# A gated dynamic convolution with a two-product layer behind it: the order of the first block's work, a load from another queue, and a third slot filled by copies

## The chip, the cores and the metric

The kernel runs on one core of a Trainium2 chip. The metric is the device time of one execution in microseconds; lower is better. Engines are named TensorE (PE, with its weight loads as PEld), VectorE (DVE), ScalarE (ACT), GpSimd (POOL) and SyncE (SP), which issues most DMAs.

## The reference, cut to what matters

```python
# x (4, 4096, 192), weight_gen (4, 4096, 8, 7): a causal convolution of 7 taps, its weights by token and head
w = exp(weight_gen - max(weight_gen, axis=-1))
w = w / (sum(w, axis=-1) + 1e-09)
x_pad = concatenate([zeros((B, 6, D)), x], axis=1)
out[b, s, h, g] = sum_k w[b, s, h, k] * x_pad[b, s + k, h, g]
# on the 16384 tokens
h = out.reshape(16384, 192) @ w_in            # w_in (192, 2048)
g = where(h >= 1, h, where(h <= -1, 0, (h + 1) ** 2 / 4))
result = g @ w_out                            # w_out (2048, 192)
```

The two weight matrices come as 64-bit floats; the kernel decodes them on the chip.

## The kernel before, in words

**Tiling.** The 16384 tokens are cut into 32 blocks of 512. A block's convolution works on a tile of 128 partitions by 4 tokens (L179, L189), so a product of one tap is an operation on 128x768. The result is turned so that the 192 channels lie on partitions, 64 to a row half: three slots c = 0, 1, 2 of 64 channels, each held twice, once in the lower and once in the upper 64 partitions, so that a pair of matmuls can work on both row halves at once. For blocks 0 and 1 slot c holds channels c*64 to c*64+127 of a row that is lengthened by its first 64 channels, and `gemm1_pair` (L378) takes the weights of slot (c + h) % 3 for row half h.

**Precision.** Every operand is split into a high and a low part (`hc`, `hl` for the activations, `whi`, `wlo` and both halves of `wo` for the weights): ScalarE copies the high part (L258, L352), VectorE or GpSimd subtracts the low part (L259, L356). The first product is 18 matmuls for a pair of 128-column slices (three slots, three passes, two row halves), the second 32 for each half.

**Order.** The whole program is under a manual schedule: each engine and each queue works in the order in which the code issues. A pair w (two slices of the 2048 hidden columns) goes through `gemm1_pair`, ScalarE's `relu` and `square` (L389, L392), VectorE's minimum and maximum `act_g` (L397), the split `split_g` (L403, L404) and, two pairs later, `gemm2_part` (L432) in two parts. A block has 8 pairs.

**The prologue** (L532 to L575). SyncE issues the loads of the softmax weights for groups 0 (block 0) and 1 (blocks 1 and 2) and the load of x for block 0 (L126, and L129 for the first two partitions, whose first rows are the zero padding that GpSimd clears at L119). `softmax` (L149 to L155) is seven operations; those of groups 0 and 1 are interleaved, with group 1's subtraction and last multiplication on GpSimd. `marks` collects instructions on which others are made to wait: the first load of the weight matrices (chunk 0 of 8, L308 and L314) waits for group 0's addition of 1e-9. `drive` (L208) keeps TensorE at work with 13 matmuls that nobody reads. `conv_summed` makes block 0's convolution as five tiles (`piece`): taps 0 and 4, 5, 6 alone, taps 1 to 3 summed on VectorE in PSUM. VectorE reads the softmax weights from a copy in PSUM (`near`, made by ScalarE, L224), GpSimd from SBUF. `again` (L169) copies a piece's first 64 channels behind its end. TensorE then turns and sums the pieces (`turn_sum`, L267): 5 pieces, 3 slots and 4 turns each, 60 in all. `split_x` makes the high and low parts of the three slots, and the first weight chunk is decoded by `cast_act`, `cast_dve`, `merge`, `high` and `low` (L327, L331, L340, L352, L356).

**After it.** `first_pairs` and `early_pair` decode one chunk for each pair while block 0 is computed; block 1's convolution runs on GpSimd in between (`wave`), each operation held until a chunk's decoding has been issued. At the last pair of block 0 (w = 7) block 1's result is turned: slots 0 and 1 before the second product's part 0, and in `edge_pair`, between the parts, slot 2. From block 2 on the turning goes over VectorE's transposition (L284) and DRAM. Block 2's convolution stands on GpSimd's queue from pair 6 on (two operations), its transposition on VectorE's at pair 11, ahead of that pair's `act_g`.

## Time and profile before

| | |
|---|---|
| median of 3 runs | 1161.32 us (1160.6 to 1161.62) |
| span of the profiled execution, first to last instruction | 1158.6 us |
| the median less this span, what lies around it | 2.7 us |
| TensorE busy | 1145.0 us, 12885 matmuls |
| VectorE, ScalarE, GpSimd busy | 834.1, 964.7, 792.5 us |
| TensorE busy from 10 to 20, 20 to 30, 50 to 60 us | 8.67, 7.01, 8.95 of 10 us |

The profiled execution is known by its span alone; its own time is put at the span and the 2.7 us around it. Busy times are of single engines that work beside each other. The span of the profile begins with the first instruction, and all places in time below are microseconds from there.

### The profile page before, as it was taken

The numbers are of one execution on the slowest core, as the hardware profiler recorded it, in microseconds if no ns is written. First come the engines' busy times: TensorE is split into PE (matmuls) and PEld (weight loads), VectorE is DVE, ScalarE is ACT, GpSimd is POOL, SyncE is SP. The second block draws the span as 40 slices with busy tenths as digits, with TensorE's granted clock in tenths as the row PEclk, the third lists the DMA queues.
The fourth block names the chain that finished last, engine by engine and source line by source line (L and its number), as shares of the span: only waits on it lengthen the run. The fifth ranks groups of instructions, "written<-read, shape, count | busy, mean of one in ns | idle before, by whom it ended". The sixth has DMA issues, their size and how long they took to land.

```text
span 1158.6 us, 32197 instructions
## 1 busy us (share of the span) xinstructions
PE 1145.0 (99%) x12885; PEld 1038.1 (90%) x12885; DVE 834.1 (72%) x1271; ACT 964.7 (83%) x1745; POOL 792.5 (68%) x511
## 2 busy tenths in 40 slices
PE   7999999999999999999999999999999999999998
PEld 5799999999999999999999999999999999999997
DVE  8887767677676776767777676776767767677664
ACT  6878888888888888888888888888888888888886
POOL 4788976667857678486686866678576785866310
PEclk9999999999999999999999999999999999999999
DMA  9422222212222212222121222222222122221100
GB/s 229 112 82 79 77 84 90 89 64 73 75 77 90 84 61 82 71 87 90 56 89 59 85 89 90 64 73 74 76 90 95 51 85 70 80 90 57 47 24 15
DMA packets 84052, 91.43 MB, mean 79 GB/s; under 512 B 5056, under 2 KB 75712, under 8 KB 83904
## 3 DMA queue, kind: packets, MB, share of 16 engines
q1 hardware_dynamic: 83904, 89.39, 24.0%
q8 instruction: 101, 1.65, 0.6%
q14 instruction: 47, 0.39, 0.1%
HBM read 64.99 MB, written 24.38 MB: 77 GB/s over the span
## 4 chain that ended last, share of the span: by engine, by line
PE 95%; ACT 2%; DMA 2%; DVE 1%; issue 0%; POOL 0%; DVEq 0%; POOLq 0%; ACTq 0%; SPq 0%
PE o L432 48%; PE psh L378 45%; DMA r<-in_moe_w_in_dram 1%; PE psx L267 1%; DMA r<-in_moe_w_out_dram 1%; PE psx L208 0%; ACT u L392 0%; DVE psh L397 0%; ACT u L389 0%; ACT gh L403 0%; DVE psw L340 0%; DVE gl L404 0%; POOL piece L189 0%; POOL acc L189 0%; ACT hc L258 0%
## 5 line engine op out<-in xcount | busy, mean ns | idle before, releaser
L432 PE MATMUL o<-wo,gh 64*128 64x384 f32 x4096 | 612.2, 355 | 1.5 <-SPq L441 1.4
L397 DVE SCALAR_TENSOR_TENSOR psh<-u,psh 128x512 f32<-128x512 f32 x512 | 354.7, 696 | 299.6 <-ACT u L392 299.4
L432 PE MATMUL o<-wo,gl 64*128 64x192 f32 x4096 | 542.7, 251 | 0.0
L432 PEld LDWEIGHTS o<-wo,gh 64*128 64x128 f32 x4096 | 421.1, 184 | 13.1 <-SPq L441 2.3
L432 PEld LDWEIGHTS o<-wo,gl 64*128 64x128 f32 x4096 | 421.3, 187 | 9.0
L389 ACT ACTIVATE u<-psh 128x512 f32<-128x512 f32 x512 | 301.5, 589 | 93.2 <-PE psh L378 91.2
L404 DVE TENSOR_TENSOR gl<-psh,gh 128x512 fp32r<-128x512 f32 x512 | 345.7, 686 | 15.3 <-ACT gh L403 1.1
L403 ACT ACTIVATE gh<-psh 128x512 fp32r<-128x512 f32 x512 | 299.2, 592 | 65.5 <-DVE psh L397 65.5
L378 PE MATMUL psh<-hc,whi 64*128 64x512 f32 x1536 | 349.8, 404 | 3.7 <-DVE wlo L356 1.9
L189 POOL TENSOR_TENSOR acc<-acc,pr 128x768 f32<-128x768 f32 x185 | 343.8, 1858 | 5.7 <-DVE head L331 2.0
L378 PE MATMUL psh<-hl,whi 64*128 64x512 f32 x1536 | 337.7, 391 | 0.0
L378 PE MATMUL psh<-hc,wlo 64*128 64x512 f32 x1536 | 337.3, 390 | 0.0
L392 ACT ACTIVATE u<-u 128x512 f32<-128x512 f32 x512 | 323.7, 632 | 16.0
L179 POOL TENSOR_TENSOR pr<-x,w 128x768 f32<-128x768 f32 x186 | 286.8, 1549 | 7.1 <-DVE psw L340 7.1
L259 POOL TENSOR_TENSOR hl<-XT,hc 128x512 fp32r<-128x512 f32 x90 | 115.4, 1297 | 221.2 <-ACT hc L258 221.2
L378 PEld LDWEIGHTS psh<-hl,whi 64*128 64x128 f32 x1536 | 173.6, 185 | 34.7 <-DVE hl L259 0.3
L378 PEld LDWEIGHTS psh<-hc,whi 64*128 64x128 f32 x1536 | 173.0, 185 | 29.4 <-DVE wlo L356 4.3
L378 PEld LDWEIGHTS psh<-hc,wlo 64*128 64x128 f32 x1536 | 174.1, 187 | 21.4
L179 POOL TENSOR_TENSOR acc<-x,w 128x768 f32<-128x768 f32 x31 | 47.9, 1547 | 72.5 <-DVE w L155 70.6
L258 ACT ACTIVATE hc<-XT 128x512 fp32r<-128x512 f32 x90 | 55.5, 618 | 0.0
L284 DVE STREAM_TRANSPOSE T<-acc 128x768 f32<-128x768 f32 x30 | 50.9, 1698 | 0.3 <-POOL acc L189 0.3
L457 DVE SCALAR_TENSOR_TENSOR osb<-o,osb 128x384 f32<-128x384 f32 x64 | 32.7, 556 | 2.7 <-ACT osb L456 2.7
(44 smaller groups left out, 188.8 us busy)
## 6 DMA issues: line engine op xcount, KB each, us to landing
x<-in_x_dram SPq DMA_DIRECT2D x28, 960.0 KB
XT<-D SPq DMA_DIRECT2D x180, 128.0 KB
out_dram<-osb SPq DMA_DIRECT2D x31, 384.0 KB
D<-T SPq DMA_DIRECT2D x30, 384.0 KB
x<-in_x_dram SPq DMA_DIRECT2D x4, 945.0 KB
w<-in_weight_gen_dram SPq DMA_DIRECT2D x15, 224.0 KB
r<-in_moe_w_in_dram SPq DMA_DIRECT2D x16, 192.0 KB
r<-in_moe_w_out_dram SPq DMA_DIRECT2D x8, 384.0 KB
```

Of the source, the lines that this page charges most:

```text
L179: held(eng.tensor_tensor(out=t, in0=xtile[:, k:k + n, :].rearrange("p j (h g) -> p j h g", h=H), in1=wt[:, gi, :, :, k:k + 1].to_broadcast ...
L189: held(eng.tensor_tensor(out=o, in0=s, in1=t, op=ALU.add))
L258: ops.append(lambda c=c: nc.scalar.activation(out=hc[:, c], in_=src[c], func=AF.Copy))
L259: ops.append(lambda c=c: lows.append(engines[c].tensor_tensor(out=hl[:, c], in0=src[c], in1=hc[:, c].bitcast(F32), op=ALU.subtract)))
L284: lambda: nc.vector.transpose(out=T.rearrange("p b c j -> p b j c"), in_=acc.rearrange("p j (r b) -> p b j r", b=R)),
L378: nc.tensor.matmul(out=pair[h][:, 0:N], lhsT=l[rows, f // 2, (c + h) % NC if b < 2 else c], rhs=r[rows, c], start=(s == 0), stop=(s == len ...
L389: nc.scalar.activation(out=u_t[i], in_=h_t[i][:, 0:N], func=AF.Relu, scale=0.5 * UNIT, bias=0.5)
L392: nc.scalar.activation(out=u_t[i], in_=u_t[i], func=AF.Square, scale=UNIT ** -0.5)
L397: nc.vector.scalar_tensor_tensor(out=pv, in0=uv, scalar=1.0 / UNIT, in1=pv, op0=ALU.min, op1=ALU.max)
L403: nc.scalar.activation(out=gh[:, 0:N], in_=gv, func=AF.Copy)
L404: nc.vector.tensor_tensor(out=gl[:, 0:N], in0=gv, in1=gh[:, 0:N].bitcast(F32), op=ALU.subtract)
L432: mm = nc.tensor.matmul(out=o_t[b][turn][:, k, 0:cols], lhsT=g_t[i][l][rows, t * P:(t + 1) * P], rhs=wo[rows, f].rearrange("p s d -> p (s ...
```

## The change

The prologue is put in another order and some of its steps are replaced.

- Block 0's x is cleared and loaded ahead of everything else; its large load is issued from ScalarE's queue, its two edge loads from SyncE's, and only then group 0's softmax weights. Group 1's weights are loaded behind the first chunk of the weight matrices, which now waits for group 0's subtraction.
- Group 0's softmax runs alone; its last multiplication writes `near` in PSUM, and ScalarE copies from there to SBUF for GpSimd. Group 1's softmax comes in between and behind the decoding of chunk 0 and the split of block 0.
- Block 0's convolution makes six pieces: taps 0 and 1 and the sum of 2 and 3 on VectorE, taps 4, 5, 6 on GpSimd. Each is turned for slots 0 and 1 alone, 8 turns, 48 in all. The drive has 9 matmuls.
- Slot 2 (channels 128 to 191, and 0 to 63) is filled by half-partition copies: the high part by ScalarE from the turned slots, the low part by GpSimd from the low parts of slots 0 and 1. Block 1's slot 2 is made in the same way in `edge_pair`.
- The second half of chunk 0's cast goes from VectorE to ScalarE.

```diff
@@ -118,12 +118,12 @@
         if halo(b):
             nc.gpsimd.memset(x_t[b][0:halo(b), 0:HALO, :], 0.0)
 
-    def load_x(b, edge=nc.sync):
+    def load_x(b, main=nc.sync, edge=nc.sync):
         t0, t, p0 = b * N, x_t[b], halo(b)
         src = bass.AP(
             tensor=xr.tensor, offset=xr[t0 + p0 * n - HALO:t0 + p0 * n - HALO + 1, :].offset,
             ap=[[n * D, P - p0], [1, (n + HALO) * D]])
-        nc.sync.dma_start(out=t[p0:P].rearrange("p j d -> p (j d)"), in_=src)
+        main.dma_start(out=t[p0:P].rearrange("p j d -> p (j d)"), in_=src)
         for p in range(p0):
             z = HALO - p * n
             edge.dma_start(out=t[p:p + 1, z:HALO + n, :], in_=xr[t0:t0 + (p + 1) * n, :])
@@ -137,7 +137,7 @@
             in_=wr[t0:t0 + nb * N, :].rearrange("(b p j) e -> p b (j e)", p=P, j=n))
         w_t[g] = t
 
-    def softmax(g, less=nc.vector, times=nc.vector):
+    def softmax(g, less=nc.vector, times=nc.vector, into=None):
         t = w_t[g]
         q = len(groups[g]) * n * H
         tv = t.rearrange("p b j h k -> p (b j h) k")[:, 0:q]
@@ -145,6 +145,7 @@
         s = sp.tile([P, 2 * n * H, 2], F32, tag="s", name="s")
         mv, sv = m[:, 0:q], s[:, 0:q, 0]
         mx, sx = (v.unsqueeze(2).to_broadcast([P, q, K]) for v in (mv, sv))
+        final = tv if into is None else into
         return [
             lambda: nc.vector.tensor_reduce(out=mv, in_=tv, axis=AX.X, op=ALU.max),
             lambda: less.tensor_tensor(out=tv, in0=tv, in1=mx, op=ALU.subtract),
@@ -152,7 +153,7 @@
             lambda: nc.vector.tensor_reduce(out=sv, in_=tv, axis=AX.X, op=ALU.add),
             lambda: nc.vector.tensor_scalar(out=sv, in0=sv, scalar1=1e-9, scalar2=None, op0=ALU.add),
             lambda: nc.vector.reciprocal(out=sv, in_=sv),
-            lambda: times.tensor_tensor(out=tv, in0=tv, in1=sx, op=ALU.mult),
+            lambda: times.tensor_tensor(out=final, in0=tv, in1=sx, op=ALU.mult),
         ]
 
     acc_t = {}
@@ -160,13 +161,10 @@
     SYNC = mybir.DependencyInfo(mybir.DependencyClass.Sync, mybir.DependencyReason.DATA)
 
     def whole():
-        return op.tile([P, n, D + Q], F32, tag="piece", name="piece", bufs=5)
+        return op.tile([P, n, D], F32, tag="piece", name="piece", bufs=6)
 
     def by_head(t):
-        return t[:, :, 0:D].rearrange("p j (h g) -> p j h g", h=H)
-
-    def again(t):
-        nc.scalar.activation(out=t[:, :, D:D + Q], in_=t[:, :, 0:Q], func=AF.Copy)
+        return t.rearrange("p j (h g) -> p j h g", h=H)
 
     def conv(b, eng, gate=None, into=None):
         g, gi = group_of[b]
@@ -213,38 +211,36 @@
                 before = None
 
 
-    def conv_summed(b):
+    near = ps_o.tile([P, 2, 512], F32, tag="o1", name="near")
+
+    def conv_pieces(b):
 
         g, gi = group_of[b]
-        wt, xtile = w_t[g], x_t.pop(b)
-        near = ps_o.tile([P, 2, 512], F32, tag="o1", name="near")
+        far, xtile = w_t[g][:, gi], x_t.pop(b)
         wn = near[:, 0, 0:n * E].rearrange("p (j h k) -> p j h k", j=n, h=H)
         sums = ps_o.tile([P, 2, 512], F32, tag="o0", name="sums")
         acc = sums.rearrange("p a d -> p (a d)")[:, 0:n * D].rearrange("p (j h g) -> p j h g", j=n, h=H)
-        nc.scalar.activation(out=wn, in_=wt[:, gi], func=AF.Copy)
+        nc.scalar.activation(out=far, in_=wn, func=AF.Copy)
 
         def times(eng, out, w, k):
             return eng.tensor_tensor(
                 out=out, in0=xtile[:, k:k + n, :].rearrange("p j (h g) -> p j h g", h=H),
                 in1=w[:, :, :, k:k + 1].to_broadcast([P, n, H, G]), op=ALU.mult)
 
-        def alone(eng, w, k):
+        def alone(eng, k):
             t = whole()
-            times(eng, by_head(t), w, k)
-            again(t)
+            times(eng, by_head(t), wn if eng is nc.vector else far, k)
             return t
 
-        def add(k):
+        def both(k):
             t = cv.tile([P, n, H, G], F32, tag="T", name="tap")
-            times(nc.vector, t, wn, k)
-            out = acc
-            if k == KV - 1:
-                own.append(whole())
-                out = by_head(own[0])
-            nc.vector.tensor_tensor(out=out, in0=acc, in1=t, op=ALU.add)
-
-        own = []
-        return alone, wn, wt[:, gi], lambda: times(nc.vector, acc, wn, 1), add, own
+            times(nc.vector, acc, wn, k)
+            times(nc.vector, t, wn, k + 1)
+            out = whole()
+            nc.vector.tensor_tensor(out=by_head(out), in0=acc, in1=t, op=ALU.add)
+            return out
+
+        return alone, both
 
 
     xT_t, xs_t, lows = {}, {}, []
@@ -259,6 +255,32 @@
             ops.append(lambda c=c: lows.append(engines[c].tensor_tensor(
                 out=hl[:, c], in0=src[c], in1=hc[:, c].bitcast(F32), op=ALU.subtract)))
         return ops
+
+    def split_turned(b, src):
+
+        hc = xt.tile([P, NC, N], F32R, tag="hc", name="hc")
+        hl = xt.tile([P, NC, N], F32R, tag="hl", name="hl")
+        xT_t[b] = (hc, hl)
+        lower, upper = slice(0, Q), slice(Q, P)
+
+        def top(c):
+            nc.scalar.activation(out=hc[:, c], in_=src[c], func=AF.Copy)
+
+        def rest(c):
+            nc.vector.tensor_tensor(out=hl[:, c], in0=src[c], in1=hc[:, c].bitcast(F32), op=ALU.subtract)
+
+        def ends(c):
+            return (lower, upper) if c else (upper, lower)
+
+        def top_end(c):
+            to, at = ends(c)
+            nc.scalar.activation(out=hc[to, 2], in_=src[c][at], func=AF.Copy)
+
+        def rest_end(c):
+            to, at = ends(c)
+            nc.gpsimd.tensor_copy(out=hl[to, 2], in_=hl[at, c].bitcast(F32))
+
+        return top, rest, top_end, rest_end
 
     def turn_sum(src, t, first, last, c):
 
@@ -531,44 +553,47 @@
     with tc.manual_schedule():
         for t in heads:
             nc.vector.memset(t, 0)
+        clear_x(0)
+        load_x(0, main=nc.scalar)
+        load_w(0)
         nc.gpsimd.memset(warm, 0.0)
         nc.scalar.activation(out=warm, in_=warm, func=AF.Exp)
-        load_w(0)
-        load_w(1)
-        clear_x(0)
-        load_x(0)
         make_identity(nc, ident)
         nc.gpsimd.tensor_copy(out=ident16, in_=ident)
         clear_x(1)
-        s0, s1 = softmax(0), softmax(1, nc.gpsimd, nc.gpsimd)
-        marks += [o() for o in s0[0:3] + s1[0:2] + s0[3:]]
-        load_weights(0, marks[6])
+        s0 = softmax(0, into=near[:, 0, 0:n * E].rearrange("p (q k) -> p q k", k=K))
+        marks += [o() for o in s0]
+        load_weights(0, marks[1])
+        load_w(1)
         load_weights(1)
         load_weights(2)
         load_x(1)
         load_weights(3)
-        run(s1[2:4])
-        alone, near, far, second, add, own = conv_summed(0)
-        src = [ps_h.tile([P, 512], F32, tag="h", name="psx") for _ in range(NC)]
-        drive(13, src[0])
-        pieces = [alone(nc.vector, near, 0), alone(nc.gpsimd, far, KV)]
-        second()
-        pieces.append(alone(nc.gpsimd, far, KV + 1))
-        add(2)
-        pieces.append(alone(nc.gpsimd, far, KV + 2))
-        add(3)
+        s1 = softmax(1, nc.gpsimd, nc.gpsimd)
+        src = [ps_h.tile([P, 512], F32, tag="h", name="psx") for _ in range(2)]
+        drive(9, src[0])
+        alone, both = conv_pieces(0)
+        pieces = [alone(nc.vector, 0), alone(nc.vector, 1), alone(nc.gpsimd, KV), alone(nc.gpsimd, KV + 1)]
+        pieces += [both(2), alone(nc.gpsimd, KV + 2)]
         cast_act(0, 0)
-        again(own[0])
-        pieces.append(own[0])
-        for k, t in enumerate(pieces):
-            for c in range(NC):
-                turn_sum(src, t, k == 0, k == len(pieces) - 1, c)
+        cast_act(0, 1)
+        order = [(k, c) for k in range(4) for c in range(2)] + [(k, c) for c in range(2) for k in (4, 5)]
+        for k, c in order:
+            turn_sum(src, pieces[k], k == 0, k == len(pieces) - 1, c)
         merge(0, 0)
-        cast_dve(0, 1)
         high(0, 0)
-        run(s1[4:6])
+        run(s1[0:2])
         low(0, 0)
-        run(split_x(0, src, [nc.vector] * NC))
+        top, rest, top_end, rest_end = split_turned(0, src)
+        top(0)
+        rest(0)
+        top_end(0)
+        top(1)
+        top_end(1)
+        rest(1)
+        rest_end(0)
+        rest_end(1)
+        run(s1[2:6])
         cast_dve(1, 2)
         merge(1, 0)
         turned1 = whole()
@@ -653,23 +678,24 @@
 
         def edge_pair(w):
             i, j = 2 * w, 2 * w + 1
-            splits = split_x(1, src1, [nc.vector] * NC)
+            top, rest, top_end, rest_end = split_turned(1, src1)
             relu(i)
             square(i)
-            run(splits[0:1])
+            top(0)
             act_g(i)
-            run(splits[1:2])
-            run(splits[2:3])
-            run(splits[3:4])
-            turn1(2)
+            rest(0)
+            top(1)
+            rest(1)
+            top_end(0)
+            top_end(1)
+            rest_end(0)
+            rest_end(1)
             split_g(i)
             relu(j)
-            run(splits[4:6])
             square(j)
             act_g(j)
             split_g(j)
 
-        at(NP - 2, lambda: again(turned1), place=4)
         at(NP - 1, lambda: turn1(0), lambda: turn1(1), place=5)
         for w in range(NS // 2 + LAGP):
             i, j = 2 * w, 2 * w + 1
```

## Rows read from the trace of the kernel before

**Rows 1.** The page: busy time of each engine; the granted clock in 40 slices.

```profile
PE 1145.0 (99%) x12885; PEld 1038.1 (90%) x12885; DVE 834.1 (72%) x1271; ACT 964.7 (83%) x1745; POOL 792.5 (68%) x511
...
PEclk9999999999999999999999999999999999999999
```

**Rows 2.** Windows: span, busy us of each engine (instructions), clock, DMA share, GB/s.

```profile
50.00:60.00 10.00, 8.95 (x81) 6.93 (x80) 7.44 (x12) 8.33 (x17) 9.78 (x6) 1.00 0.00 0
```

**Rows 3.** The chain of waits up to 80 us: start, duration, what.

```profile
2.74 5.57 PE psx L208 x13
8.31 6.55 PE psx L267 x60
14.86 2.49 PE psh L378 x18
...
52.05 1.85 POOL piece L189
```

**Rows 4.** Timeline of VectorE: start, duration, operation, idle before it and releaser.

```profile
2.83 0.39 DVE L149 TENSOR_REDUCE m<-w 128x32 f32<-128x224 f32 x1 [0.35 <-DMA w<-in_weight_gen_dram]
...
4.60 0.38 DVE L152 TENSOR_REDUCE s<-w 128x32 f32<-128x224 f32 x1
5.01 0.77 DVE L153 TENSOR_SCALAR s<-s 128x32 f32<-128x32 f32 x1
...
6.20 0.39 DVE L155 TENSOR_TENSOR w<-w,s 128x224 f32<-128x224 f32 x1
...
7.07 0.95 DVE L227 TENSOR_TENSOR piece<-x,near 128x768 f32<-128x768 f32 x1
...
11.64 0.96 DVE L244 TENSOR_TENSOR piece<-sums,tap 128x768 f32<-128x768 f32 x1
...
13.26 0.19 DVE L153 TENSOR_SCALAR s<-s 128x64 f32<-128x64 f32 x1
...
14.65 1.89 DVE L259 TENSOR_TENSOR hl<-psx,hc 128x512 fp32r<-128x512 f32 x3 [0.21 <-ACT hc L258]
16.46 0.61 DVE L331 TENSOR_SCALAR head<-r 128x768 f16<-128x768 bf16 x1
```

**Rows 5.** Timeline of SyncE's queue: DMA issues.

```profile
0.74 0.88 SPq L135 DMA_DIRECT2D w<-in_weight_gen_dram  x2
...
2.21 0.52 SPq L129 DMA_DIRECT2D x<-in_x_dram  x2
5.80 1.36 SPq L308 DMA_DIRECT2D r<-in_moe_w_in_dram  x2
```

**Rows 6.** Timeline of GpSimd, the first 12 us.

```profile
0.78 1.05 POOL L119 MEMSET x<- 2x1152 f32 x1
...
2.40 0.29 POOL L541 CAST ident<-ident 128x128 bf16<-128x128 f32 x1
...
6.92 4.54 POOL L227 TENSOR_TENSOR piece<-x,w 128x768 f32<-128x768 f32 x3 [1.18 <-DMA x<-in_x_dram]
```

**Rows 7.** Timeline of ScalarE, the softmax and the split of block 0.

```profile
3.68 0.39 ACT L151 ACTIVATE w<-w 128x224 f32<-128x224 f32 x1 [1.44 <-DVE w L150]
...
14.02 1.58 ACT L258 ACTIVATE hc<-psx 128x512 fp32r<-128x512 f32 x3 [0.42 <-PE psx L267]
```

**Rows 8.** Timeline of TensorE between the two parts at block 1.

```profile
56.11 0.25 PE L432 MATMUL o<-wo,gl 64*128 64x192 f32 x2
...
57.45 0.44 PE L432 MATMUL o<-wo,gh 64*128 64x384 f32 x2
```

**Rows 9.** Timelines of GpSimd, VectorE and TensorE at the transposition of block 2.

```profile
71.98 3.77 POOL L189 TENSOR_TENSOR acc<-acc,pr 128x768 f32<-128x768 f32 x2
...
76.31 1.57 DVE L284 STREAM_TRANSPOSE T<-acc 128x768 f32<-128x768 f32 x1
...
79.14 1.29 DVE L404 TENSOR_TENSOR gl<-psh,gh 128x512 fp32r<-128x512 f32 x2
...
80.61 0.42 PE L378 MATMUL psh<-hc,whi 64*128 64x512 f32 x2
```

## The prediction

> **What bounds the kernel now.** I read the page first: TensorE is busy for 1145.0 of 1158.6 us [rows 1], so at most 13.6 us can come from its idle time, and a change in the prologue is worth what it moves the moment from which TensorE runs without gaps. The windows say where that is: the stretch from 50 to 60 us is the last one with a gap worth naming, 8.95 of 10 us busy [rows 2]; behind it the matmuls follow each other. The chain of waits shows what leads there [rows 3]. TensorE's 13 driving turns (L208) come first, then the 60 turns of the first block's pieces, 6.55 us at 0.11 us each, without a gap; so those turns set when the first block can be split. Then 18 matmuls of the first pair, and far later VectorE and ScalarE hand each other the decoding of the weights, until GpSimd's last addition for block 1 (52.05 to 53.90), for which TensorE waits. The VectorE timeline [rows 4] has to be read for idle entries: behind the first subtraction of the split (14.65) none stands there through the decoding of the first chunks, so VectorE is the engine that carries a delay of the front through to it, and the start of its cast of chunk 1 (16.46) is the mark by which I measure the front.
>
> The profile's execution is known by its span, 1158.6 us; the median of the runs, 1161.32, is 2.7 us more, which lies around the span. I sum against the span and add the same 2.7.
>
> **Softmax of the first block.** Call T the moment at which VectorE starts the first maximum; it was 2.83 [rows 4], when the load issued at 0.74 [rows 5] had landed, 2.09 us after its issue. In the new order SyncE issues the two small edge loads (0.52 together) of x ahead of this load. One of them writes where the GpSimd memset of x has written (partition 1, rows 2 to 9, over a memset of rows 0 to 5), so it waits for that memset, 0.78 to 1.83 [rows 6]; the memset goes ahead of the other one now and ends near 1.8. The load of the weights stands behind on SyncE's queue: an edge of 0.26 us behind 1.8 [rows 5], then the load at about 2.13 instead of 0.74. That is 1.39 later, T = 4.2. It then shares the DMA engines with the 945 KB of x, which before stood behind it. No row shows two queues together: the lower bound is nothing, the upper one that it waits until x has passed; x, issued between 1.62 and 2.21 with 336 KB ahead of it, was there by 6.92 [rows 5, 6], so for the part of it that is still to come at 2.5 I take 1.2. I choose 0.3, nearer to the row of a load alone, as the load is an eighth of x: T = 4.5, bounds 4.2 to 5.4.
>
> From T to the first product it was 4.24 us (2.83 to 7.07). Of this 0.53 goes, since the sum no longer stands behind the second group's maximum (the exponential ended at 4.07 [rows 7], the sum began at 4.60); 0.58 goes, since the addition of 1e-9 took 0.77 beside GpSimd's subtraction and 0.19 by itself (13.26); and 0.42 goes, nearly all of 6.59 to 7.07, where ScalarE's copy stood, since the last multiplication writes PSUM itself. About 2.7 is left: first product at T + 2.7. ScalarE's copy for GpSimd is now behind the multiplication, so GpSimd starts at T + 3.1; three products of 1.5 [rows 6] end at T + 7.7. It started at 6.92, held by x; at T = 4.5 it starts at 7.6, so the earlier x from ScalarE's queue (its issue at 0.74 instead of 1.6) releases nobody.
>
> **Six pieces, 48 turns.** VectorE makes three of them with five operations at 0.87 to 0.97 (7.07 to 12.60 held six [rows 4]): T + 2.7 to T + 7.3. TensorE turns 48 times at 0.11: the first piece is there at T + 3.7, four pieces end at T + 7.3, slot 0 of the last two at T + 8.2 and slot 1 at T + 9.1. The producers and the turns are level, so both bind. The five copies of the extra 64 columns on ScalarE go; they stood beside TensorE's queue of turns and cost nothing.
>
> **Split by half copies.** ScalarE does four copies instead of three, at 0.53 [rows 7]: T + 8.3 to T + 10.4, then the exponential of the second group, some 0.5 between 0.39 for half the columns and 0.53, to T + 10.9. VectorE does two subtractions instead of three (0.63 each [rows 4]), but the maximum and the sum of the second group are now in its path here, some 0.6 each (0.38 at half the size, 4.60), and it waits for the exponential: sum to T + 11.5, addition (0.19) and reciprocal (0.5) to T + 12.2, then the cast of chunk 1. At T = 4.5 that is 16.7 against 16.46: **+0.2**. GpSimd's two half copies fill slot 2 by about T + 11.3 and the 18 matmuls end by T + 11.9, 0.9 earlier than 17.3 [rows 3], but the decoding waits for VectorE, so this is worth nothing. The weights of chunk 0 are issued behind the subtraction, at T + 0.85 = 5.35 against 5.80 [rows 5]; the load of the second group (0.44) goes behind them. No cast of before waited for them (no idle entry at 16.46), and this gives nothing; if the cover went, each chunk would be late by the 0.4 of that load at most.
>
> **The clock of TensorE.** [...] With 9 driving turns TensorE is busy from 2.74 to 6.6 only, 3.9 us, and then idle until T + 3.7 = 8.2. So its turns may start at the lower level, at 0.22 instead of 0.11. Below: nothing, the clock is up. Above: a stretch of turns as long as the 5.57 us of driving at half pace, 25 turns at 0.11 more, 2.5 us with the gaps that they fill. I take the 1.7 us of driving that is gone, run as turns at half pace, seven of them: **+0.8**. [...]
>
> **Block 1.** Four turns and the wait before them go: part 1 of the second product starts at 57.45 where part 0 began its last turns at 56.11 [rows 8], so TensorE gains 1.3. But two half copies are put on GpSimd, and GpSimd is in one piece from 52.05 on to the end of block 2's convolution at 75.75 [rows 3, 9]. For it waits VectorE's transposition (76.31), behind it two minima and the two subtractions that end at 80.43, and for these banks the pair at 80.61, with 0.2 to spare. No row shows a copy of 512 columns on GpSimd. Below: 0.29, the cast of 128 [rows 6]; above: 1.51, a product of 768 [rows 6]. I take 0.65, nearer to the cast, which is of its kind. The transposition then starts at 75.8 + 1.3 = 77.1, 0.8 later than now; the pair at 80.61 comes 0.6 later than the front's own shift, and the 1.3 is lost in a stall of some 1.9 us in front of it. **+0.6**, bounds -0.1 to +2.3.
>
> **Sum:** 0.2 + 0.8 + 0.6 = +1.6 us, a span of 1160.2, a time of 1162.9. A measurement of this kernel can tell about 0.2%, 2.3 us, from no change; so I forecast no change, on the slow side.
>
> **Rivals.** *The turns start at the lower clock (slower).* Place: the gap between the ninth driving turn and the first piece. It decides from the point at which T exceeds about 2.9, since then TensorE is idle after 6.6. Price: 2.5 instead of 0.8, +3.3, 1164.6. For it: the pace of all 13 driving turns. Against it: the window of 50 to 60 holds a gap of 1 us too [rows 2], and the granted clock is full there.
>
> *GpSimd has room.* If the copies are short, or the transposition is not what the pair at 80.61 waits for, the 1.3 us of block 1 stay: 0.2 + 0.8 - 1.3 = -0.3, 1161.0. Against it: no idle entry on GpSimd from 53.83 to 75.75.
>
> *The softmax is not late (faster).* If the edge load does not hold SyncE, T is near 2.9, the front is 1.4 earlier, the pieces follow the driving turns with no gap, and the weights start 2 us earlier. With block 1's gain that is -2.7, 1158.6. Against it: the overlap of edge and memset stands in the code.
>
> *The load from ScalarE's queue does nothing.* This is part of the forecast: x is not what comes last, unless T is small.
>
> **How the numbers follow.** Forecast 0.36, the clock 0.27, room on GpSimd 0.16, softmax not late 0.21. Slower by over 0.2%: the clock and 0.03 of the forecast (its T near 5.4), 0.30. Faster: 0.17 of the last and 0.03 of the room (both with a T near 4.2 and no loss by the clock), 0.20. Within 0.2%: 0.50. The range goes from 1159.3, which cuts most of the early softmax, to 1165.3, the clock's case with half a microsecond more of T. The forecast's own range is 1161.5 to 1164.
>
> **What would show it.** Right: VectorE's first maximum near 4.5, the load of its weights issued behind 2 us; a gap on TensorE in front of the first turn and the first turns 0.2 apart; the cast of chunk 1 near 17.5; no wait between the two parts at block 1; GpSimd's two copies at 57 and a gap on TensorE of nearly 2 us near 80. Wrong: a maximum at 2.9, turns that follow the driving ones, or TensorE without a gap from 57 on, each of which is one of the rivals.

## The result, and the profile after

The changed kernel takes 1166.91 us (median of 4 runs, 1166.54 to 1168.55) against 1160.96 us of the kernel before on the same chip: 1.0052 of it, 95% interval 1.0039 to 1.0065. It is slower by 6 us, beyond the range that was given. The profiled execution has a span of 1164.7 us (1158.6 before) in a time of 1166.54.

The page of the changed kernel, the lines that answer to [rows 1], and its DMA queues (packets, MB, share):

```profile
PE 1146.9 (98%) x12865; PEld 1035.5 (89%) x12865; DVE 831.8 (71%) x1267; ACT 964.4 (83%) x1742; POOL 794.6 (68%) x515
...
PEclk8999999999999999999999999999999999999999
...
q1 hardware_dynamic: 83764, 88.42, 23.9%
...
q10 hardware_dynamic: 140, 0.97, 0.2%
```

TensorE has about the same to do and 4.2 us more idle time, and a first slice in which the granted clock is not full. The new queue q10 carries one thing, the 945 KB of x. The VectorE timeline of the changed kernel, for [rows 4]:

```profile
5.91 0.39 DVE L150 TENSOR_REDUCE m<-w 128x32 f32<-128x224 f32 x1 [3.42 <-DMA w<-in_weight_gen_dram]
...
9.14 1.82 DVE L226 TENSOR_TENSOR piece<-x,near 128x768 f32<-128x768 f32 x2 [0.54 <-ACT w L223]
...
17.06 0.69 DVE L270 TENSOR_TENSOR hl<-psx,hc 128x512 fp32r<-128x512 f32 x1 [1.80 <-ACT hc L267]
19.65 0.69 DVE L270 TENSOR_TENSOR hl<-psx,hc 128x512 fp32r<-128x512 f32 x1 [1.89 <-ACT hc L277]
20.26 0.61 DVE L153 TENSOR_REDUCE s<-w 128x64 f32<-128x448 f32 x1
...
21.60 0.54 DVE L353 TENSOR_SCALAR head<-r 128x768 f16<-128x768 bf16 x1
```

Its SyncE queue, for [rows 5], then TensorE's timeline, for [rows 3]:

```profile
0.74 1.30 SPq L129 DMA_DIRECT2D x<-in_x_dram  x2
2.09 0.36 SPq L135 DMA_DIRECT2D w<-in_weight_gen_dram  x1
6.74 1.36 SPq L330 DMA_DIRECT2D r<-in_moe_w_in_dram  x2
```

```profile
2.74 4.02 PE L206 MATMUL psx<-ident 128*128 128x512 bf16 x9 [2.74 <-POOL ident L562]
10.15 7.13 PE L289 MATMUL psx<-ident,piece 128*128 128x128 f32 x48 [3.38 <-DVE piece L226]
```

Two windows of TensorE (window, length, busy us and instructions, granted clock, DMA share, GB/s) show where its clock was at half:

```profile
10.40:13.70 3.30, 3.30 (x17) 0.50 1.09 260
20.50:27.30 6.80, 5.74 (x23) 0.50 1.08 250
```

The cast of chunk 1, the mark of the prediction, is at 21.60 instead of 16.46, 5.14 later. By stages of the two VectorE timelines and of TensorE's turns:

| stage | before | after | moved | forecast |
|---|---|---|---|---|
| to the first maximum (T) | 2.83 | 5.91 | +3.08 | +1.67 |
| T to the first product | 4.24 | 3.23 | -1.01 | -1.54 |
| first product to the last turn's end | 7.79 | 8.14 | +0.35 | -1.39, +0.8 for the clock |
| last turn to the cast of chunk 1 | 1.60 | 4.32 | +2.72 | +1.50 |

The four add up to 5.14 where 1.04 had been forecast. The shift stays as it is through the decoding: the last merge of the weights is at 54.06 for 48.97, 5.09 later. Block 1's part then adds 0.8 (a pair at 85.00 starts at 90.93).

### The profile page after: what moved, and what is told of

Its sections match the earlier page's. It is cut to its first block, busy times and chain, and to the rows that moved or that the text cites. A ratio compares the mean times of both kernels' runs of the same rounds, so it can differ in the third digit from the quotient of the medians.

```text
span 1164.7 us, 32159 instructions
## 1 busy us (share of the span) xinstructions
PE 1146.9 (98%) x12865; PEld 1035.5 (89%) x12865; DVE 831.8 (71%) x1267; ACT 964.4 (83%) x1742; POOL 794.6 (68%) x515
## 4 chain that ended last, share of the span: by engine, by line
PE 92%; ACT 3%; DVE 2%; issue 1%; DMA 1%; DVEq 0%; POOL 0%; SPq 0%; ACTq 0%; POOLq 0%
PE o L454 48%; PE psh L400 44%; ACT u L414 1%; DVE psh L419 1%; ACT gh L425 1%; ACT u L411 1%; PE psx L289 1%; DVE gl L426 0%; DMA r<-in_moe_w_in_dram 0%; DMA w<-in_weight_gen_dram 0%; ACT whi L374 0%; DVE psw L362 0%; ACT wo L374 0%; DVE w L151 0%; DVE hl L270 0%
## 5 line engine op out<-in xcount | busy, mean ns | idle before, releaser
L454 PE MATMUL o<-wo,gh 64*128 64x384 f32 x4096 | 603.7, 355 | 1.0 <-DVE osb L479 0.9
L454 PE MATMUL o<-wo,gl 64*128 64x192 f32 x4096 | 525.6, 251 | 0.0
L454 PEld LDWEIGHTS o<-wo,gl 64*128 64x128 f32 x4096 | 399.0, 187 | 10.7
L454 PEld LDWEIGHTS o<-wo,gh 64*128 64x128 f32 x4096 | 393.5, 184 | 12.9 <-DVE osb L479 1.3
L400 PE MATMUL psh<-hc,whi 64*128 64x512 f32 x1536 | 327.3, 405 | 5.0 <-DVE wlo L378 2.2
L400 PE MATMUL psh<-hl,whi 64*128 64x512 f32 x1536 | 314.8, 392 | 0.6 <-DVE hl L270 0.6
L400 PE MATMUL psh<-hc,wlo 64*128 64x512 f32 x1536 | 314.4, 391 | 0.0
L400 PEld LDWEIGHTS psh<-hl,whi 64*128 64x128 f32 x1536 | 154.1, 186 | 37.0 <-DVE hl L270 1.4
L400 PEld LDWEIGHTS psh<-hc,whi 64*128 64x128 f32 x1536 | 153.7, 185 | 32.1 <-DVE wlo L378 4.3
L400 PEld LDWEIGHTS psh<-hc,wlo 64*128 64x128 f32 x1536 | 154.4, 187 | 21.9
```

The lines of the kernel that those rows point to most:

```text
L400: nc.tensor.matmul(out=pair[h][:, 0:N], lhsT=l[rows, f // 2, (c + h) % NC if b < 2 else c], rhs=r[rows, c], start=(s == 0), stop=(s == len ...
L454: mm = nc.tensor.matmul(out=o_t[b][turn][:, k, 0:cols], lhsT=g_t[i][l][rows, t * P:(t + 1) * P], rhs=wo[rows, f].rearrange("p s d -> p (s ...
```

## Experiments

Each stage of the table got runs of its own. Ratios are against the kernel before, run on the same chip between the others; the names in brackets are those by which the expectations refer to each other. A trace shows one execution; where that is far from the median of its kernel, the text gives its time.

**1. Is it the order on SyncE's queue, or x on a queue beside it?** First the softmax weights ahead of the edges, x still on ScalarE's queue (e1_w_first):

```diff
-        clear_x(0)
-        load_x(0, main=nc.scalar)
         load_w(0)
+        clear_x(0)
+        load_x(0, main=nc.scalar)
```

> The changed kernel with one step moved: the load of group 0's softmax weights is issued first on SyncE, the two edge loads of x behind it. Theory (the loss of 5.95 us has three parts in front, the late softmax, the low clock of TensorE and a split in which ScalarE and VectorE take turns, and one at block 1): the first maximum goes back from 5.91 to about 2.9, everything up to the cast of chunk 1 moves by 3.0 or a little more, 1163.5 to 1164. Rival (the clock alone is the loss): TensorE's gap in front of its turns shrinks from 3.4 to about 0.3 us, the low clock goes, 1161 to 1162. Rival (the load of x from ScalarE's queue holds up whatever shares the DMA engines): the first maximum stays behind 4, 1165 or more.

Then the same with `load_x(0)`, all of x behind the weights on SyncE (e5_x_behind):

> The changed kernel with block 0's large load of x back on SyncE's queue, behind the load of group 0's softmax weights (both are issued ahead of the two edge loads); all else stays. Theory after the first four runs (the softmax weights wait for x because x runs on a queue of its own beside them; where they stand on SyncE's queue does not matter, 6.19 against 5.91): first maximum near 2.8, turns near 7.1, weights issued near 3.7; 3 us come back and the low clock of the turns with them, 1162 to 1163.5. Rival (something else holds the softmax weights, such as the start of the transfers): first maximum stays near 6, 1166.5 or more.

The first maximum of the two, in this order:

```profile
6.19 0.39 DVE L150 TENSOR_REDUCE m<-w 128x32 f32<-128x224 f32 x1 [3.71 <-DMA w<-in_weight_gen_dram]
```

```profile
2.84 0.39 DVE L150 TENSOR_REDUCE m<-w 128x32 f32<-128x224 f32 x1 [0.36 <-DMA w<-in_weight_gen_dram]
...
6.87 1.82 DVE L226 TENSOR_TENSOR piece<-x,near 128x768 f32<-128x768 f32 x2 [1.34 <-DMA x<-in_x_dram]
...
15.82 0.69 DVE L270 TENSOR_TENSOR hl<-psx,hc 128x512 fp32r<-128x512 f32 x1 [1.90 <-ACT hc L277]
...
17.77 0.54 DVE L353 TENSOR_SCALAR head<-r 128x768 f16<-128x768 bf16 x1
```

Issued at 0.75, 1.3 sooner than in the changed kernel, the weights landed no sooner as long as x went beside them: 1166.77 us, 1.0048 (1.0035 to 1.0062). With x behind them on the same queue they were there at 2.84: 1164.13 us, 1.0028 (1.0017 to 1.0038), slower than the 1162 to 1163.5 expected. So with x beside them the memset and the edges, on which the forecast had put 1.39 of T, cost nothing that is seen; x on a queue of its own cost all of the 3.08. Whether it would cost as much when issued from ScalarE's queue only after the weights have landed was not tried, nor the edges first with all loads on SyncE. Putting x behind the weights moves the cast by 3.83 in the trace, which is that of the lowest of eight times (1162.13 to 1165.86), and gives back nearly half of the loss between the medians.

**2. Why so long?** In both kernels with two queues the small load was there only near 6 us. The two loads have about as many rows (128 of 896 bytes, 126 of 7680), so if the queues were served in turn row by row, the small one would end with the large one, and sooner if x came in more and smaller rows. That was a theory to test. x in two and in five loads per row (e16_x_halves, e17_x_fifths):

```diff
-        main.dma_start(out=t[p0:P].rearrange("p j d -> p (j d)"), in_=src)
+        for m in range(cuts):
...
+            main.dma_start(out=t[p0:P, m * step:(m + 1) * step].rearrange("p j d -> p (j d)"), in_=src)
```

> The changed kernel with the load of x still on ScalarE's queue, but as two loads of half a row each (five of ten tokens), one behind the other. In the changed kernel the softmax weights (112 KB in rows of 896 bytes, 128 of them) landed at 5.9 beside x (945 KB in rows of 7680 bytes, 126 of them): the two queues hold about as many packets. Theory A (the two queues are served in turn, packet by packet, so the small load ends when as many packets of x have passed): with half rows it ends behind half of x, some 0.55 of the stretch from 2.2 to 5.7, so the first maximum starts near 4.4 (4.0 to 4.8), the cast of chunk 1 1.5 earlier (20.1) and the time falls by 1 to 1.5 to 1165.6. Theory B (x, issued first, passes as a whole, or the engines are shared by bytes): the first maximum stays at 5.7 to 6.3, and the time at 1166.9.

> The same with five loads of two tokens a row (1536 bytes). Theory A: the small load ends behind a fifth of x, 0.29 of that stretch, near 3.3 and no sooner than the 2.83 of the kernel before plus the 1.4 that its issue is later, so the first maximum starts at 4.2 (3.4 to 4.4); what the five issues on ScalarE cost (some 0.5 each) stands ahead of the first exponential and binds nothing before 4.8. Theory B: 5.7 to 6.3 again.

```profile
6.05 0.39 DVE L153 TENSOR_REDUCE m<-w 128x32 f32<-128x224 f32 x1 [3.57 <-DMA w<-in_weight_gen_dram]
```

```profile
6.50 0.39 DVE L153 TENSOR_REDUCE m<-w 128x32 f32<-128x224 f32 x1 [4.01 <-DMA w<-in_weight_gen_dram]
```

With twice the rows T is 6.05, with five times 6.50, above theory B's 6.3 too (1167.23 and 1167.53 us, 1.0056 and 1.0058). Theory A falls: the number of rows does not set T. The queues' packets (packets, MB, share; the 126 rows of x stand there as 140) show two pictures. In the changed kernel, first from 2.5 to 4.0 us and then from 4.0 to 5.5, q1 being SyncE's queue and q10 that of x:

```profile
q10 hardware_dynamic: 77, 0.59, 94.0%
...
q10 hardware_dynamic: 43, 0.22, 38.7%
q1 hardware_dynamic: 146, 0.12, 25.2%
```

And in e1_w_first, from 3.5 to 5.0:

```profile
q10 hardware_dynamic: 66, 0.51, 81.0%
q1 hardware_dynamic: 63, 0.05, 9.4%
```

In the changed kernel the small load, issued at 2.09, moves nothing before 4.0, when 97 of x's 140 packets have gone; issued at 0.75, together with x, it goes beside x about one packet for one (63 and 66) and lands no sooner (6.19). With x in fifths 64 packets of x still move between 6.0 and 7.0, after the last of the small load, and T is 6.50 all the same. So it need not wait for the whole of x, and neither theory describes all four kernels; how the engines share the two queues stays open. What these kernels have in common is a T of 5.91 to 6.50 with x on the other queue.

**3. The clock.** More driving turns in the changed kernel (e2_drive20):

```diff
-        drive(9, src[0])
+        drive(20, src[0])
```

> The changed kernel with 20 driving turns instead of 9, so that TensorE has no gap ahead of its first turn. Theory: the softmax stays as late as it is (first maximum at 5.9); the 48 turns take 5.3 us instead of 7.1 and the pair at half pace behind 23 us goes, so 1.5 to 2.5 us come back: 1164.4 to 1165.4. Rival (the clock alone is the loss): nearly all comes back, 1161 to 1162. Rival (VectorE's chain binds, the clock is beside it): 1166.5 or more.

```profile
2.74 5.92 PE L206 MATMUL psx<-ident 128*128 128x512 bf16 x20 [2.74 <-POOL ident L562]
10.22 5.55 PE L289 MATMUL psx<-ident,piece 128*128 128x128 f32 x48 [1.55 <-DVE piece L226]
```

The 48 turns take 5.55 instead of 7.13: the gap of 3.38 behind nine driving turns had cost 1.58. That size is one draw: in the four other traces with nine driving turns and x on ScalarE's queue (experiments 1, 2 and 4) the turns take 6.88, 8.00, 7.20 and 6.78. The cast of chunk 1 comes at 20.11, 1.5 sooner, and the time is 1164.83 us, 1.0028 (1.0016 to 1.0040), as expected. The last merge, though, is at 53.40, only 0.66 sooner, in a trace with the highest of six times (1165.71) and with the granted clock at half from 19.4 to 26.1 and from 33.1 to 39.7.

**4. The half copies.** ScalarE's half copies read from `hc` in SBUF instead of from PSUM (e3_ends_high):

```diff
-            nc.scalar.activation(out=hc[to, 2], in_=src[c][at], func=AF.Copy)
+            nc.scalar.activation(out=hc[to, 2], in_=hc[at, c].bitcast(F32), func=AF.Copy)
```

> The changed kernel, with ScalarE's two half copies of the high part read from the finished high part in SBUF instead of the turned slot in PSUM. Theory (ScalarE's read of a PSUM bank waits for VectorE's subtraction from the same bank): the second half copy of slot 0 no longer waits 0.75 us for the subtraction, and VectorE's second subtraction starts about 1.2 us earlier; 0.8 to 1.2 us come back, 1165.7 to 1166.1. Rival (TensorE's turns at low clock set the split's end): under 0.3 us, 1166.6 or more.

ScalarE in the changed kernel, for [rows 7], and then with this edit:

```profile
16.43 0.60 ACT L267 ACTIVATE hc<-psx 128x512 fp32r<-128x512 f32 x1 [1.76 <-PE psx L289]
17.79 0.59 ACT L277 ACTIVATE hc<-psx 64x512 fp32r<-64x512 f32 x1 [0.75 <-DVE hl L270]
18.40 0.60 ACT L267 ACTIVATE hc<-psx 128x512 fp32r<-128x512 f32 x1
19.02 0.59 ACT L277 ACTIVATE hc<-psx 64x512 fp32r<-64x512 f32 x1
```

```profile
16.41 0.60 ACT L267 ACTIVATE hc<-psx 128x512 fp32r<-128x512 f32 x1 [1.42 <-PE psx L289]
17.04 0.63 ACT L277 ACTIVATE hc<-hc 64x512 fp32r<-64x512 f32 x1
17.70 0.60 ACT L267 ACTIVATE hc<-psx 128x512 fp32r<-128x512 f32 x1
18.33 0.63 ACT L277 ACTIVATE hc<-hc 64x512 fp32r<-64x512 f32 x1
```

In the changed kernel the half copy waits for VectorE's subtraction of the same bank (0.75), and VectorE's second subtraction for the half copy of its bank (1.89); from SBUF neither does, and the second subtraction starts at 18.33 instead of 19.65. Only half of that reaches the cast of chunk 1 (20.95 for 21.60), since the second group's sum now waits 0.57 for its exponential. VectorE's first product had waited in the same way for ScalarE's copy out of `near` (0.54 above). All three waits stand where two engines read one bank; no run lets them read it together, so what would happen then is not shown. The median hardly moves, 1166.42 us, 1.0047 (1.0033 to 1.0061), by less than the 0.8 to 1.2 expected; in the trace, that of the highest of four times (1167.23), T was 6.23, and the last merge is at 54.14, where it was at 54.06.

**5. The second group's softmax.** Sum, addition and reciprocal behind the first merge of chunk 1, on top of e5_x_behind and e3_ends_high (e9_tail_late):

```diff
-        run(s1[2:6])
+        run(s1[2:3])
         cast_dve(1, 2)
         merge(1, 0)
+        run(s1[3:6])
```

> The changed kernel with x behind the softmax weights on SyncE's queue (first maximum near 2.84), the half copies of the high part read from SBUF, and the sum, addition and reciprocal of the second group's softmax behind the cast of chunk 1 and its first merge. Theory A (what is left of the loss at the front lies in VectorE's own order: the copies that wait for its PSUM banks, and the second group's softmax ahead of the decoding): against x behind the weights alone (cast of chunk 1 at 17.77, 1164.1 us) the SBUF copies give 1.0 and the three steps 1.35, so the cast of chunk 1 starts near 15.4, 1.1 ahead of the kernel before; the merges follow 2.4 earlier (last of them near 47.7) and the time is 1161.7 (1160.5 to 1162.5), still with block 1's +0.7 and with whatever a low clock behind a gap takes. Theory B (the decoding is bound elsewhere, by ScalarE's casts or by the landing of the weights): the cast of chunk 1 starts near 15.4 but the merges stay within 0.5 of 50.1 and the time within 0.7 of 1164.1.

The cast of chunk 1 starts at 15.15, as expected, 1.3 ahead of the kernel before; the last merge at 49.13, not 47.7, and the time is 1161.95 us, 1.0012 (1.0002 to 1.0022). The three steps, 1.34, now stand between the two merges of chunk 1 (15.79 and 17.89): they had been moved by one place, not out of VectorE's way.

An earlier run with x behind the weights, the half copies from SBUF and block 1's half copies of the low part on VectorE, but the second group's softmax where the change has it (e7_combo), was expected at 1158.5 to 1160 and missed it: 1163.70 us, 1.0018 (1.0008 to 1.0027). In its trace x came late, with the first product at 8.25 where e5_x_behind, with the same order of issue, has 6.87, and the cast of chunk 1 is at 18.51.

**6. Block 1 by itself**, put into the kernel before; once as changed, and once with VectorE instead of GpSimd for the low half copies (e4_edge_alone, e8_edge_dve):

```diff
         def edge_pair(w):
-            splits = split_x(1, src1, [nc.vector] * NC)
+            top, rest, top_end, rest_end = split_turned(1, src1)
...
-        at(NP - 2, lambda: again(turned1), place=4)
```

> The kernel before with block 1's part of the change alone: slot 2 of block 1 by half copies, no turn between the two parts of the second product. Theory (GpSimd comes later with block 2's convolution and TensorE gives the 1.3 us back): no wait between the two parts, a gap on TensorE of some 2 us between 70 and 82, 0.5 to 1 us slower than before, 1161.5 to 1162. Rival (the 1.3 us stay): 1159.5 to 1160.

> The kernel before with block 1's part of the change, and its two half copies of the low part on VectorE instead of GpSimd. Theory (GpSimd's 1.3 us of copies delay block 2's transposition): GpSimd ends block 2's convolution where it did, near 75.8, the gap at the pair near 81 shrinks, 0.4 to 1 us faster than before, 1160.2 to 1160.8. Rival (the copies on GpSimd do not matter): the same as with them, 1161.8.

TensorE in the first of them, and its VectorE:

```profile
69.85 0.44 PE L458 MATMUL o<-wo,gh 64*128 64x384 f32 x2 [0.86 <-DVE osb L483]
```

```profile
62.11 1.91 DVE L150 TENSOR_TENSOR w<-w,m 128x448 f32<-128x448 f32 x1
...
77.61 1.70 DVE L310 STREAM_TRANSPOSE T<-acc 128x768 f32<-128x768 f32 x1 [1.32 <-POOL acc L189]
```

1161.80 and 1161.58 us, both 1.0006 (0.9997 to 1.0015), 0.7 us over the kernel before if anything. TensorE is early by 0.97 at first (57.70 for 58.67), though the front, whose code is the same, is 0.35 late in this trace (last merge at 49.32 for 48.97); then it waits 0.86 for block 0's output copies: the third softmax's subtraction now falls on one of GpSimd's operations and takes 1.91 (0.71 before), and the minima and copies behind it are late. With the copies on VectorE the transposition comes at 76.81 without a wait, but the subtraction takes 2.20, TensorE waits 0.87 for the same copies, and nothing is won. So GpSimd's half copies are not all that takes the 1.3 us: without them the output copies do. Moving that softmax away by one pair was to show it (e12_group2_late):

```diff
-                where = [(7, 4), (7, 4), (8, 4), (8, 4), (10, 4), (10, 4), (11, 2)]
+                where = [(8, 4)] * 4 + [(10, 4), (10, 4), (11, 2)]
```

> The kernel before with block 1's part of the change alone (1161.8 us, pair 14 at 86.16 against 85.0, TensorE idle for 0.86 behind block 0's output copies), and the maximum and subtraction of the third softmax one pair later. Theory A (VectorE and GpSimd collide: the subtraction took 1.91 instead of 0.71 beside GpSimd's multiplications, and this pushes the minima, the output copies and TensorE): the subtraction takes under 1.0 or stands behind the output copies, TensorE's gap near 69.85 falls under 0.3, and what is left is the transposition behind GpSimd (wait 1.3): pair 14 at 85.6 or earlier, 1161.0. Theory B (the output copies are bound by the chain of squares and minima, whatever VectorE does between): the gap stays within 0.3 of 0.86, pair 14 within 0.3 of 86.16, 1161.8. Theory C: the addition of GpSimd takes the collision elsewhere and its end moves from 77.6, with the transposition.

```profile
71.50 0.68 PE L458 MATMUL o<-wo,gh 64*128 64x384 f32 x2 [2.70 <-DVE osb L483]
```

None of the three: 1163.65 us, 1.0020 (1.0010 to 1.0029). The subtraction still took 1.57, and the exponential, now right behind it on ScalarE, held that engine for 2.96, with the output copies behind it; and from 71.6 to 74.9 us, behind TensorE's gap, the granted clock is 0.50, so the time is not the wait's alone. It shows that TensorE's wait moves with this softmax, not how to be rid of it.

**7. What is left of the new front.** All of this undone: x behind the weights, 13 driving turns, block 1 as before, copies from SBUF, the softmax tail as in 5; first with the weights of chunk 0 released behind the reciprocal, then behind the subtraction as in the change (e10_front_alone, e11_front_best):

```diff
-        drive(9, src[0])
+        drive(13, src[0])
...
-        load_weights(0, marks[1])
+        load_weights(0, marks[5])
```

> The same front, but with 13 driving turns as before, the first chunk's weights issued behind the reciprocal of the first softmax (so that they do not share the DMA engines with x), and block 1 split as before the change (third slot by turns). Theory A (the six pieces and half copies are a gain by themselves, and the queue of x, the clock, the order on VectorE and block 1 took it away): the driving turns end near 8.3, the turns start behind them without a gap over 0.5 and at 0.11 each, no stretch at a lower granted clock in the first 50 us, the cast of chunk 1 near 15.0, merges 1 to 1.5 earlier than before (last near 47.7), and 1159.8 us (1159.2 to 1160.6), under the kernel before. Theory B (the 48 turns and half copies are worth nothing, since the decoding behind them is bound by ScalarE's casts and weights): merges within 0.4 of before (48.97) and 1161.0 to 1161.6.

> The front of e10_front_alone (x behind the softmax weights on SyncE, 13 driving turns, half copies from SBUF, the second group's sum behind the first merge of chunk 1, block 1 split as before) with the first chunk's weights issued behind the first subtraction again instead of behind the reciprocal. Theory A (the cast of chunk 1 waited 1.29 for the weights there): the wait goes, the cast starts near 15.2 as in e9_tail_late, and the merges follow 0.9 to 1.0 earlier than there (last of those shown 50.10 there, near 49.1 here), 1160.3 us if the low stretch of TensorE's clock stays at 6.8 us or less. Theory B (x shares the DMA engines with the weights and the first product comes later by as much): first product at 6.9 instead of 6.2, last merge within 0.4 of 50.1, and 1161.1. In both a stretch at the lower clock is expected behind TensorE's gap at 16 to 19.5, which costs some 1.7 us of the merges.

1161.06 us, 0.9998 (0.9990 to 1.0006), and 1160.35, 0.9999 (0.9990 to 1.0008). Released late, the weights let the first product start at 6.20 (6.84 otherwise, both waiting for x), but then the cast of chunk 1 waits 1.29 for them, at 16.19 instead of 15.09. The gain expected of the first did not come; the second's median is the 1160.3 of its theory A, but its runs can't be told from those of the kernel before. Next, 11 driving turns in TensorE's gap ahead of the second pair (e14_fill):

> The same kernel with 11 more driving turns (into an unused bank) between the first and the second pair, where TensorE waited for the high and the low part of chunk 1 (1.06 and 1.07 in e9_tail_late). Theory A (the low stretch from 19 to 23 or 26.5 comes of TensorE's gap in front of it, and it costs the merges behind it): granted clock full from 17 to 30, the second pair's matmuls at 0.23 each, the merges behind 28 come 1.5 earlier than without the turns (near 47.6 for the last), and the time 1159.3 us (1158.6 to 1160.3), below the kernel before. Theory B (the stretch does not come of that gap): a stretch of 3.4 us or more between 17 and 30 all the same, merges and time within 0.4 of e11_front_best. Theory C (the driving turns delay the second pair, since TensorE would have been ready sooner): its first matmul starts more than 0.3 later and the time is above e11_front_best.

1161.41 us, 1.0004 (0.9995 to 1.0013). Its trace is that of the highest of eleven times (1164.48), and of another kind than expected, though the loads are issued as in the run before:

```profile
8.96 1.82 DVE L229 TENSOR_TENSOR piece<-x,near 128x768 f32<-128x768 f32 x2 [3.41 <-DMA x<-in_x_dram]
```

x landed 2.1 later here, beside the weights of chunk 0. Between 17 and 30 us the clock is full, as theory A has it, but that is worth little: from the first merge of chunk 2 to that of chunk 3 it takes 7.67 (24.11 to 31.78) for 7.84 without the turns (20.41 to 28.25). So the granted clock of 0.50, there from 19.5 to 23, goes with no more than 0.17 in this stretch. What the turns would give with x in time, this trace does not show. Last, the second group's load and softmax put back where they were, and chunk 0's weights behind the addition again, the six pieces and half copies kept (e15_both_softmax):

```diff
-        marks += [o() for o in s0]
+        marks += [o() for o in s0[0:3] + s1[0:2] + s0[3:]]
...
-        run(s1[0:2])
+        run(s1[4:6])
```

> The front of e11_front_best (six pieces, 48 turns, half copies from SBUF, 13 driving turns, all loads on SyncE), but the second group's load and softmax again where the kernel before has them: load behind the first one, maximum, exponential and sum ahead of the products, addition and reciprocal between the first chunk's high and low part; block 1 split as before. Theory A (six pieces and half copies are a gain of about one microsecond at the front, and the second group's softmax, moved into VectorE's way behind the turns, is what takes it): the cast of chunk 1 starts near 15.0, bound by the end of the turns as in e11_front_best (15.09), but no sum, addition and reciprocal (1.35) stand between the two merges of chunk 1, so the last of the merges comes near 48.0 (49.36 there, 48.97 before) and the time is 1160.0 us (1159.3 to 1160.8). Theory B (the decoding behind is bound by ScalarE and the pairs, and a shorter front is worth nothing): the last merge within 0.4 of 48.97 and 1160.9 to 1161.4. Theory C (the second group's softmax holds up the first products, as it stands ahead of them): the first product starts later than 7.2 and the cast of chunk 1 near 16.

TensorE (two lines of its timeline) and ScalarE in this kernel:

```profile
8.68 5.55 PE L292 MATMUL psx<-ident,piece 128*128 128x128 f32 x48 [1.63 <-DVE piece L229]
...
17.04 0.51 PE L403 MATMUL psh<-hl,whi 64*128 64x512 f32 x2
18.61 1.38 PE L403 MATMUL psh<-hc,whi 64*128 64x512 f32 x2 [1.06 <-ACT whi L377]
```

```profile
17.58 0.60 ACT L414 ACTIVATE u<-psh 128x512 f32<-128x512 f32 x1 [1.64 <-PE psh L403]
18.07 0.48 ACT L377 ACTIVATE whi<-psw 128x384 fp32r<-128x384 f32 x1
```

1160.52 us, 0.9996 (0.9987 to 1.0005): no gain that can be told, and a last merge at 49.36, not 48.0. The turns end at 14.23, 0.63 before those of [rows 3] (14.86), but the first pair ends at 17.55, where it ended at 17.35: the chain of copy, half copy, copy, subtraction and half copy takes 3.3 from the last turn to the pair's end, three whole splits took 2.5. ScalarE's next high part stands behind an operation that waits for that pair. The median lies in theory A's range, but the merges are theory B's, with the first pair as the bound; and the first product at 7.67 and the cast of chunk 1 at 15.92 are where theory C had them, though it was x that the product waited for (0.71) and not the softmax.

## Why the prediction was wrong

**The step that failed first** is the price of the second queue: "the lower bound is nothing, the upper one that it waits until x has passed", T = 4.5, at most 5.4. The upper end was nearly what the trace shows, and my figure for it was too low by 0.5: T was 5.91. I took 0.3 for what x costs the small load because that is an eighth of x, but none of it moved before 4.0, when 97 of x's 140 packets had gone (experiment 2). The 1.39 for the memset and the edges stands in the trace as an issue (2.09), and is worth nothing as long as x goes beside it (6.19 without it, experiment 1). T missed by 1.41.

**The first product** at T + 2.7 was T + 3.23: the softmax ended as forecast, at T + 2.69, but that VectorE and ScalarE both read `near`, and so VectorE waits 0.54 for ScalarE's copy, was not seen.

**The clock.** Place and pace were right, those of the first rival: a gap of 3.38, and first turns at half pace, 17 matmuls in the 3.30 us at a granted clock of 0.50, then 35 in 3.60 at 1.00. The term was 0.8, seven turns at half pace, an estimate of mine; the runs showed 1.58 (7.13 for 5.55), inside its bounds. A gap does not bring it every time: 2.50 in e7_combo was followed by 48 turns in 5.55 at a granted clock of 1.00, 2.13 in e14_fill by 7.13. Not in the sum were the stretches at half clock behind later gaps (20.5 to 27.3): the changed kernel itself loses nothing by them up to the last merge (5.14 late at the cast of chunk 1, 5.09 there), but in experiment 3, with two of them, 0.8 of the 1.5 that the front won was gone by then.

**The split.** "ScalarE does four copies instead of three, at 0.53: T + 8.3 to T + 10.4", back to back; they took 16.43 to 19.61, 3.2 for 2.1, with VectorE in turns (experiment 4). The term from the last turn to the cast of chunk 1 was +1.50 and came to +2.72. The second group's softmax in VectorE's way was priced rightly within it: 1.3, against 1.34 in the trace (20.26 to 21.60).

**Block 1** was +0.6 and came to 0.84 in the changed kernel's trace; by itself (experiment 6) it is not clear of nothing. The number was near in part by luck. TensorE did win its 1.3 (the pair at 58.67 comes at 62.45, with the front 5.09 late). The forecast lost it in one place, behind the transposition that waits for GpSimd, with a stall of 1.9; there it lost 0.76 (81.39 to 90.93, two pairs, is 9.54 for 8.78), and 1.38 was lost sooner, at block 0's output copies (71.23 to 77.00, one pair, is 5.77 for 4.39), which the forecast does not name. With no wait for GpSimd (experiment 6, second kernel) the 1.3 us are lost all the same at these copies, near 70, so the condition of "GpSimd has room" would not have kept them.

**The sum** would have been 1.04 + 0.6; the four misses of the front are 1.41 + 0.53 + 0.94 + 1.22 = 4.10 (the third with all of the turns' stage), and 1.04 + 4.10 + 0.8 = 5.94 stands against 5.95 between the medians. The four add up by construction, as each stage begins where the one before it ends in the same two traces; what the agreement shows is that the delay of the front is handed on whole. Of the rivals, "the turns start at the lower clock" is the one that came about, with a T that none of them had.

No version tried beats the kernel before: the best three, 0.9996 to 0.9999, can't be told from it.

## What to carry to other kernels

A load on another queue is not only an earlier start: here 112 KB that landed for a start at 2.84 with the large load behind them were there only for 5.91 to 6.50 with it on another queue. So price a small load that something waits for as if the large one went first. When an operation reads PSUM, list who else reads that bank: in this program the second reader waited 0.54, 0.75 and 1.89, and half copies made from SBUF had neither of the last two waits. A step taken out of a queue's front has to go somewhere: the second group's sum, addition and reciprocal, put behind the last subtraction, stood in the way of the decoding for 1.34.

## What the runs showed of the hardware

- With all loads on SyncE, the first product, held by x, started at 6.20, 6.84, 6.87, 6.90, 7.67, 8.25 and 8.96 us in the seven kernels told of here (experiments 1, 5 and 7); 6.84 and 8.96 have the same order of issue, and so have 6.87 and 8.25. The five that issue chunk 0's weights behind the subtraction, at 3.6 to 3.7, have runs that spread by 2.4 to 4.4 us; the two that issue them at 5.1 and 5.6 (6.20 and 7.67) have runs that spread by 1.5 and 1.4. That the late landing of x makes the difference was not tested.
- Thirteen driving turns took 5.57 us in the kernel before and 4.31, 4.47, 4.51 and 5.10 in those of experiment 7, with a granted clock that reads 1.00 from 2.7 to 7.2 us in all five: that column does not show the difference.
- The half copies of 64x512 on GpSimd took 0.60 to 0.64 each at both blocks of the changed kernel, as estimated; two on VectorE beside GpSimd's work took 2.22.
- VectorE's subtraction of the third softmax took 0.71 in the kernel before, 1.57 to 2.20 in the three kernels of experiment 6 and 1.92 in the changed one. In all five it ended 0.48 or 0.49 after the end of the GpSimd operation that was under way when it began.
